# A product and a sum moved forward in the hand-written order of a group step (GFNet mixing and SwiGLU on one core)

## The chip, the cores and the metric

The kernel runs on one core of one Trainium2 chip, in fp32 throughout. The metric is the device time of one execution, in microseconds (us), as the median of several runs. Before the change it is 2811.93 us (three runs, 2810.69 to 2812.69).

## What is computed

Eight images of 3008 tokens and 256 channels are filtered along the token axis in the frequency domain, and each resulting token goes through a gated feed-forward block of width 1536.

```python
X = np.fft.rfft(x, axis=1)                       # x: 8 x 3008 x 256
y = np.fft.irfft(X * (filt_r + 1j * filt_i)[None], n=3008, axis=1)
t = y.reshape(24064, 256)
g = t @ w_gate                                   # 256 x 1536
out = (g * (1 / (1 + np.exp(-g))) * (t @ w_val)) @ w_out
```

## The kernel before

TensorE multiplies, and the other engines feed it. Each image (b, 0 to 7) is worked off in twelve group steps. A group step is one pair (k, g): k is one of four chunks of the image's tokens, g one of three thirds of the 1536 hidden channels. Ninety-six steps of 25 to 30 us each make up nearly all of the time.

**Inside a group step.** The tokens of a chunk are split in four blocks (0 to 3), and the products are saved by a scheme like Strassen's: instead of all block products, sums of blocks are multiplied and the results are recombined.

- P0 to P3 and Q0 to Q3 are the eight products of single blocks. Pi and Qi share one PSUM bank, k_i. Q0 opens bank k0 and P0 adds to it; so for blocks 0, 1 and 2, while P3 opens k3 and Q3 adds to it.
- A, B and E with two digits are products of sums of two blocks (18 of them), in banks a_ij and e_ij. Each product is two matmuls of 128x188, seen in the trace as four rows named wk, wa or we (line 1123); four W rows (wA, wF, wG, line 1220) are one of the seven output projections W1 to W7 of the group before.
- Between them come small operations. ScalarE copies: f_i (line 1138) is the negative of k_i after its first product, c_i (line 1142) is k_i after both, m (line 1158) copies an A bank, g and u (line 1165) are the Silu. VectorE: x and s (line 1145) form a bank's starting value from a k bank and an f (x03 and s13 both read k3, which P3 has opened; s13 writes the bank that A13 then adds to, s01 that of A01), y and e (line 1152, by the helper at line 327) do the like from a k bank and a c (e13 writes the bank that E13 adds to), l (line 1162, helper at line 323) subtracts, h and v (line 1170) multiply by the Silu, and o (helper at line 320, or ScalarE at line 1232) adds a finished projection to the output tile. GpSimd: D (differences of two f) and S (sums of hidden tiles for the projections).

**What sets the order.** SCHEDULE (lines 88 to 96) is the order of a group step, written out by hand: a list of tokens which the loop at line 1487 goes through once in each step, each token issuing its instructions to their engines. All are kept in the order of the program on their engine. A token with a prime (') belongs to the group of the step before. ORDER (line 107) picks the product tokens out of it and so sets in which slot of the weight tile each product's weights lie; PIECES (line 114) are the ranges of slots that are reloaded together, and the first holds slots 0 to 6, which end with Q2.

Between the products lie tokens of other work: t and i tokens (the last stage of the inverse transform for the next chunk, and output stores of image 0), x and z tokens (output stores and transposes), n tokens (sums of blocks for the next step), and b0 to b7, the eight parts of a burst: one piece of the spectrum of the image after. In images 1 to 6, steps 0 to 3 have a burst of the kind "quads" (line 733), steps 4 to 10 one of the kind "fours" (line 813), and the last step, in images 0 to 5, a "first_fold" (line 727). A burst's first parts put matmuls (wqa at line 743; wqc and wqb at lines 823 and 835) on TensorE between W2 and Q1; ScalarE copies their banks out (lines 754, 858 and 849), VectorE adds and subtracts (helpers at lines 320 and 323, line 853), SP and ScalarE store the result. Image 7 has no burst. Image 0 has instead the preparation of tables and weights, whose pieces are issued at fixed places of the list (tick_at, line 562).

Some work is tied to a token by name and goes where the token goes. For P0: keep_filter in steps 0 to 3 of image 1 (FILTER_AT, line 103), and in image 0 load_back in step 8 and reload_y in steps 3 to 8 (lines 1420 and 1424). All of these are DMA issues on SP.

Of the kernel before, what the change touches and what calls it, by code (L numbers as in the profile page):

```python
# [85 lines left out]


SCHEDULE = """
Q0 o3' z1.o' t4.2' W2 b0 f0 S00' S01' i0 b1 b2 x0.o' t0.0 x1.o' i1 Q1 t0.1 x2.o' P3 x3.o' f1 t4.3'
W1 x4.o' S10' x03 S11' D01 i2 i3 i4 s13 b3 x5.o' P1 o1 b4 t0.2 P0 o2 z0.o c1 i5 A13 g1 c0 S20' Q2  # L90
S21' g0 y01 m13 t1.0 h0 f2 s01 W6 t1.1 h1 x23 D02 P2 o6 D12 A01 t0.3 i6 c2 i7 B13 i8 g2 i9 n3' m01
i10 S30' t1.2 i11 x02 W7 S31' g13 y12 y02 B01 h13 o7 t1.3 t2.0 s02 s12 g01 h2 b5 Q3 t2.1 h01 e12
A02 y23 W4 e02 b6 y03 m02 g3 A12 o4 z2.o t2.2 E12 m12 B02 t2.3 l12 b7 E02 u12 e13 g02 t3.0 h3 s23
l02 B12 v12 E13 t3.1 h02 u02 A23 n2 l13 g12 v02 W5 s03 e23 h12 e01 m23 A03 o5 z3.o u13 E23 t3.2 m03
v13 E01 l23 e03 t3.3 t4.0 l01 u23 B23 v23 u01 E03 n1 t4.1 v01 g23 B03 l03 W3 h23 g03 u03 h03 v03
""".split()
# [1478 lines left out]
```

## Time and profile before

| quantity | value |
|---|---|
| median of three runs | 2811.93 us |
| profiled execution, device time | 2810.07 us |
| its span in the profile | 2808.3 us |
| TensorE clock granted | 0.999 |
| TensorE matmul rows | 15832 |
| mean row of wa, wk, we (128x188) | 323, 326, 323 ns |
| mean row of wA (128x376) | 481 ns |
| TensorE wk at line 1123 waiting for ScalarE's f | once, 1.7 us |
| TensorE wA at line 1220 waiting for VectorE's burst sum | three times, 1.9 us together |

The matmul rows overlap: one starts while the one before it still drains, so the distance from start to start, not the row's length, is what a product costs. Four rows of a product start 0.16 us apart in the unbroken parts, four rows of W 0.32 apart. In a timeline, rows of one kind that follow each other are joined ("x8" for two products of four), with their start, and the time from there to the end of the last. PEld rows are weight loads, which run beside matmuls. Behind the arrow in square brackets stands which work the engine waited for. "lent" is the name under which buffers of a shared room appear that a burst uses.

### The profile page before, as it was taken

Reading aid. Unit: us, or ns where it says so; the run is one execution under the profiler, and the core shown is the slowest. Engines: PE = TensorE matmul, PEld = TensorE weight load, DVE = VectorE, ACT = ScalarE, POOL = GpSimd, SP = SyncE. Lnnn points to the kernel's source line nnn. Section 1 sums busy time; section 2 is a strip of 40 time slices with the busy share of each in tenths; the row PEclk is TensorE's granted clock in tenths of the full one; section 3 lists DMA queues with packets and bytes.
Section 4 is the critical chain, followed back from the end, with each engine's and each line's share of the span. In section 5 each row is a group of like instructions: output and inputs, shape, how many; then the busy total and the mean of one; then the engine's idle time right before and its main releaser. Section 6 shows DMA issues by size and latency. Waiting matters only on the chain.

```text
span 2808.3 us, 49267 instructions
## 1 busy us (share of the span) xinstructions
PE 2773.1 (99%) x15832; PEld 2307.1 (82%) x15832; DVE 2048.3 (73%) x4675; ACT 1560.7 (56%) x4170; POOL 1580.9 (56%) x1689
## 2 busy tenths in 40 slices
PE   8999999999999999999999999999999999999998
PEld 6777888788888888888888888888888888888887
DVE  7888767777677766777767677777677767666666
ACT  5775455555555555555555555555555555555554
POOL 5886575465546565446554566455555455545544
PEclk9999999999999999999999999999999999999999
DMA  8778877777676776677767676668766677654543
GB/s 215 243 260 278 283 238 238 261 235 261 185 221 201 254 247 185 211 227 229 244 191 222 219 249 218 205 193 260 240 211 200 215 236 230 187 154 146 153 138 82
DMA packets 385272, 608.53 MB, mean 217 GB/s; under 512 B 198876, under 2 KB 268444, under 8 KB 384840
## 3 DMA queue, kind: packets, MB, share of 16 engines
q1 hardware_dynamic: 366202, 574.39, 65.2%
q10 hardware_dynamic: 16174, 25.50, 3.5%
q0 software_dynamic: 2640, 5.51, 0.8%
q8 instruction: 128, 2.10, 0.3%
q14 instruction: 128, 1.05, 0.1%
HBM read 484.65 MB, written 118.12 MB: 215 GB/s over the span
## 4 chain that ended last, share of the span: by engine, by line
PE 91%; POOL 2%; DVE 2%; ACT 1%; issue 1%; DMA 0%; POOLq 0%; ACTq 0%; DVEq 0%; SPq 0%
PE wa L1123 25%; PE wk L1123 17%; PE wA L1220 17%; PE we L1123 12%; PE wG L1220 8%; PE wF L1220 4%; PE pd L1026 3%; PE wqc L823 1%; PE wqb L835 1%; PE wqa L743 1%; POOL h L323 1%; POOL out_dram L1205 0%; PE pa L905 0%; PE pc L980 0%; DMA lent<-later_tbl 0%
## 5 line engine op out<-in xcount | busy, mean ns | idle before, releaser
L1123 PE MATMUL wa<-y_t,wt_t 128*128 128x188 f32 x4464 | 879.6, 323 | 5.0 <-ACT m L1158 2.4
L1123 PEld LDWEIGHTS wa<-y_t,wt_t 128*128 128x128 f32 x4464 | 745.9, 190 | 83.7 <-ACT wa L1149 9.5
L1123 PEld LDWEIGHTS wk<-y,wt_t 128*128 128x128 f32 x2976 | 494.1, 190 | 114.2 <-issue 34.0
L1123 PE MATMUL wk<-y,wt_t 128*128 128x188 f32 x2976 | 576.5, 326 | 2.1 <-ACT f L1138 1.7
L320 POOL TENSOR_TENSOR h<-h 128x376 f32<-128x376 f32 x190 | 182.9, 984 | 687.0 <-DVE h L1170 687.0
L323 POOL TENSOR_TENSOR h<-h 128x376 f32<-128x376 f32 x572 | 559.7, 1000 | 15.4 <-DVE h L320 15.2
L1220 PE MATMUL wA<-h,wo_t 128*128 128x376 f32 x1532 | 550.9, 481 | 5.9 <-DVE o L320 2.0
L1123 PE MATMUL we<-y_t,wt_t 128*128 128x188 f32 x2232 | 433.0, 323 | 2.1 <-ACT we L1154 1.5
L323 POOL TENSOR_TENSOR D<-f,f 128x376 f32<-128x376 f32 x288 | 280.9, 986 | 246.1 <-ACT f L1138 234.6
L323 DVE TENSOR_TENSOR we<-we,m 128x376 f32<-128x376 f32 x576 | 319.0, 555 | 125.1 <-ACT m L1158 60.9
L1123 PEld LDWEIGHTS we<-y_t,wt_t 128*128 128x128 f32 x2232 | 368.6, 190 | 6.1 <-DVE we L327 3.9
L1220 PEld LDWEIGHTS wA<-h,wo_t 128*128 128x128 f32 x1532 | 275.7, 190 | 113.9 <-POOL h L323 5.7
L1158 ACT COPY m<-wa 128x376 f32<-128x376 f32 x576 | 272.2, 473 | 83.5 <-PE wa L1123 79.6
L1165 ACT ACTIVATE u<-we 128x188 f32<-128x188 f32 x576 | 188.6, 327 | 171.7 <-DVE we L323 164.3
L1165 ACT ACTIVATE g<-wa 128x188 f32<-128x188 f32 x576 | 187.2, 326 | 164.8 <-PE wa L1123 158.1
L327 DVE SCALAR_TENSOR_TENSOR y<-wk,c 128x376 f32<-128x376 f32 x480 | 246.0, 538 | 40.3 <-ACT c L1142 23.0
L1220 PE MATMUL wG<-h,wo_t 128*128 128x376 f32 x768 | 274.0, 479 | 0.0
L1142 ACT COPY c<-wk 128x376 f32<-128x376 f32 x288 | 136.3, 473 | 212.8 <-PE wk L1123 212.8
L1154 ACT COPY we<-y 128x376 f32<-128x376 f32 x480 | 222.0, 480 | 18.8 <-DVE h L1170 13.9
L1138 ACT ACTIVATE f<-wk 128x376 f32<-128x376 f32 x288 | 139.9, 486 | 165.7 <-PE wk L1123 128.5
L1170 DVE TENSOR_TENSOR h<-wa,g 128x188 f32<-128x188 f32 x576 | 198.3, 345 | 34.8 <-ACT g L1165 34.5
L1170 DVE TENSOR_TENSOR h<-we,u 128x188 f32<-128x188 f32 x576 | 197.8, 344 | 28.9 <-ACT u L1165 17.5
(195 smaller groups left out, 3560.2 us busy)
## 6 DMA issues: line engine op xcount, KB each, us to landing
wt_t<-w_all SPq DMA_DIRECT2D x174, 896.0 KB
wt_t<-w_all SPq DMA_DIRECT2D x174, 768.0 KB
lent<-filter SPq DMA_DIRECT2D x36, 1024.0 KB
quads<-lent SPq DMA_DIRECT2D x96, 256.0 KB
d<-lent ACTq DMA_DIRECT2D x84, 256.0 KB
lent<-quads SPq DMA_DIRECT2D x144, 128.0 KB
lent<-raw SPq DMA_DIRECT2D x144, 128.0 KB
t<-d SPq DMA_DIRECT2D x114, 128.0 KB
```

The lines of the kernel that those rows point to most:

```text
L320: return eng.tensor_tensor(out=dst, in0=a, in1=b, op=ALU.add)
L323: return eng.tensor_tensor(out=dst, in0=a, in1=b, op=ALU.subtract)
L327: return nc.vector.scalar_tensor_tensor(out=dst, in0=a, scalar=-1.0, in1=b, op0=ALU.mult, op1=ALU.subtract)
L1026: pin(nc.tensor.matmul(out=rows, lhsT=self.t4[k, i][:, j, ts(cb, 128)], rhs=cols, start=j == 0, stop=True, skip_group_check=True))
L1123: pin(nc.tensor.matmul(out=ps[:, z], lhsT=self.wt[:, SLOT[p], z], rhs=rhs, start=start and z == 0, stop=True, skip_group_check=True))
L1138: pin(act.mul(self.small(f"f{i}", f"f{i}", 1), t[f"k{i}"], -1.0))
L1142: pin(act.copy(out=self.small(f"c{i}", f"c{i}", 1), in_=t[f"k{i}"]))
L1154: pin(act.copy(out=self.bank(f"e{at}"), in_=t[f"y{at}"]))
L1158: pin(act.copy(out=self.small(f"m{at}", "m", 4), in_=t[f"a{at}"]))
L1165: pin(act.activation(out=self.small(op, "g", 3, 1)[:, 0], in_=ps[:, 1], func=AF.Silu))
L1170: pin(v.tensor_tensor(out=dst, in0=ps[:, 0], in1=g, op=ALU.mult))
L1220: pin(nc.tensor.matmul(out=self.tiles[at], lhsT=wo_t[:, JB * q + i, WO[p], :], rhs=self.hs[i][:, HID[p]], start=start and i == 0, stop=Tru ...
```

## The change

Two tokens of SCHEDULE are moved; nothing else in the file differs. P0 goes from behind t0.2, where it followed P3, W1' and P1, to directly behind Q1 and so ahead of P3. e13 goes from behind b7, E02 and u12 to directly behind l12, ahead of the burst's last part b7.

```diff
-Q0 o3' z1.o' t4.2' W2 b0 f0 S00' S01' i0 b1 b2 x0.o' t0.0 x1.o' i1 Q1 t0.1 x2.o' P3 x3.o' f1 t4.3'
-W1 x4.o' S10' x03 S11' D01 i2 i3 i4 s13 b3 x5.o' P1 o1 b4 t0.2 P0 o2 z0.o c1 i5 A13 g1 c0 S20' Q2
+Q0 o3' z1.o' t4.2' W2 b0 f0 S00' S01' i0 b1 b2 x0.o' t0.0 x1.o' i1 Q1 P0 t0.1 x2.o' P3 x3.o' f1 t4.3'
+W1 x4.o' S10' x03 S11' D01 i2 i3 i4 s13 b3 x5.o' P1 o1 b4 t0.2 o2 z0.o c1 i5 A13 g1 c0 S20' Q2
...
-A02 y23 W4 e02 b6 y03 m02 g3 A12 o4 z2.o t2.2 E12 m12 B02 t2.3 l12 b7 E02 u12 e13 g02 t3.0 h3 s23
+A02 y23 W4 e02 b6 y03 m02 g3 A12 o4 z2.o t2.2 E12 m12 B02 t2.3 l12 e13 b7 E02 u12 g02 t3.0 h3 s23
```

The number of instructions is the same on every engine, and so are the PSUM banks. TensorE's products go Q0, W2', burst, Q1, P0, P3, W1', P1, A13, Q2 where they went Q0, W2', burst, Q1, P3, W1', P1, P0, A13, Q2. P0 adds to bank k0, which f0 reads after Q0 alone; so P0 must come after f0 has read it. The slots of P0, P3 and P1 in the weight tile change places within the first piece. On VectorE the order changes where b7 issues something there: e13 is then ahead of it.

## The prediction

> **What bounds the kernel now.** I read the page's busy table and chain of waits first, then TensorE's waits and those of its weight loads, then the timeline at one group step of each kind, and added up only what TensorE stands still for.
>
> ```profile
> PE 2773.1 (99%) x15832; PEld 2307.1 (82%) x15832; DVE 2048.3 (73%) x4675; ACT 1560.7 (56%) x4170; POOL 1580.9 (56%) x1689
> ...
> PE 91%; POOL 2%; DVE 2%; ACT 1%; issue 1%; DMA 0%; POOLq 0%; ACTq 0%; DVEq 0%; SPq 0%
> ```
>
> TensorE is busy for 99% of the span and is 91% of the chain. The change alters no instruction of it, so all that can move is where it stalls. The busy figure hides stalls of a few tenths; the weight loads' waits name them:
>
> ```profile
> PEld wa L1123 <- DVE wa L1145: 7.7, 17, 1.2
> ...
> PEld wk L1123 <- ACT lent L754: 6.3, 24, 0.4
> ...
> PEld we L1123 <- DVE we L327: 3.9, 14, 0.5
> ...
> PEld wk L1123 <- ACT f L1138: 2.8, 3, 1.9
> PEld wA L1220 <- PE wk L1123: 2.7, 3, 0.9
> ```
>
> The second row is P3 (24 steps: the four of images 1 to 6 whose bursts are quads) waiting until ScalarE has copied out the burst's bank. The third is E13 waiting for e13. The fifth (W1, three times) is on TensorE's own row 1.9 us put down to VectorE's burst sum of L320. The first is mostly A01 waiting for s01. These are idle times of the load queue, some of it cover for matmuls still running; the stall itself is read from starts. In a quads step (image 4):
>
> ```profile
> 1521.96 1.75 PE L1123 MATMUL wk<-y,wt_t 128*128 128x188 f32 x8
> 1522.16 1.07 ACT L754 COPY lent<-wqa 128x512 f32<-128x512 f32 x2 [1.89 <-PE wqa L743]
> 1522.80 0.61 PEld L1123 LDWEIGHTS wk<-y,wt_t 128*128 128x128 f32 x4 [0.23 <-ACT lent L754]
> 1523.54 1.43 PE L1220 MATMUL wA<-h,wo_t 128*128 128x376 f32 x4
> ```
>
> Q1 and P3 (the x8) take 1.58 us from start to W1's start (1521.96 to 1523.54). In image 7, which has no bursts, the same pair takes 1.27 (2478.20 to 2479.47), in a step with the other burst, a fours, 1.43 (1634.57 to 1636.00). And the far end of that same kind of step, here the first of image 4:
>
> ```profile
> 1470.91 0.80 PE L1123 MATMUL wk<-y,wt_t 128*128 128x188 f32 x4
> 1472.06 1.54 PE L1123 MATMUL wa<-y_t,wt_t 128*128 128x188 f32 x8 [0.35 <-DVE wa L1145]
> ```
>
> P2 needs 0.64 (half of 1.27), A01 starts 1.15 after it: a 0.51 us stall for s01. VectorE runs without a hole from 1465.08 (the burst's first subtraction) to the end of s01 at 1472.01. So in these steps VectorE, not TensorE, sets when A01 starts.
>
> **What the skill says.** "TensorE: Matmul & The Clock Gate" (Architectural detail) says TensorE's queue can pull weight loads ahead of running matmuls while VectorE and ScalarE are strictly first in, first out. The trace agrees: a product that never waited follows its predecessor at 0.64 us; one that waited pays about 0.10 more, since its second load was not ahead (E13 below: 0.75 to its successor). "PSUM — Partial Sum Buffer" (PSUM bank collisions raise a hardware error) says two engines must not be on one bank at once: hence P0, which adds into k0, must wait for f0's read of k0. The trace of before has no such wait in nearly all steps, since P0 came late.
>
> **The change, part by part.**
>
> P0 ahead of P3, fours (42 steps; in 30 of them, five of each image, ScalarE has three copies of the burst to make ahead of W1). Q1 to P1 takes 2.77 us (1634.57 to 1637.34) against 2.53 in image 7 (2478.20 to 2480.73). The excess of 0.24 holds 0.10 at Q1, which restarts behind the burst and keeps that, and 0.14 at W1, whose loads begin when ScalarE's second copy (L849) ends at 1635.96. P0 puts 0.64 of work ahead, so W1 no longer waits. 30 x 0.14 to 0.16 = 4.5 us less. What could take it back: P3, and with it x03 and s13, come 0.64 later. VectorE was busy until x03 at 1636.37, and P3 will end near 1636.60, so x03 moves by 0.4 to 0.5. s13 is still early for A13, and s01 would end at 1641.2 instead of 1640.78, with A01 at 1641.65: 0.4 of room. The saving stays.
>
> P0 ahead of P3, quads (24 steps). 1.58 less 1.27 less Q1's 0.10 is 0.21 of stall at P3; P0's 0.64 covers it: 24 x 0.21 = 5.0 us, first. But x03 starts no earlier: P3 ends near 1523.98 against the old 1523.5, so x03 starts at about 1524.25 instead of 1524.11, and VectorE's unbroken row to s01 moves 0.13 later. TensorE arrives 0.21 earlier at a wait that ends 0.13 later. In the first step of each image that is +0.13; in the third the room is 0.08 (s01 ends 1529.11, A01's loads begin 1529.17), so +0.15; in the second and fourth about 0 (Q2 behind an accumulator read, and A01, take it). 6 x 0.28 = +1.7 us net instead of -5.0.
>
> Steps 1 to 3 of image 1. Here W1 waits for VectorE's burst sum at a fixed time, 0.63 each (TensorE's row says 1.9 for three). P0 is done in that time: up to -1.9. VectorE's row is next; as TensorE was late here A01 has more room, so I take -1.6.
>
> e13 ahead of the last burst sum. In 14 quads steps E13 waits. In the third of image 4, A02 to E13 is 0.85 and E13 to its successor 0.75 (1537.53, 1538.38, 1539.13) where 0.64 each is due: 0.32 lost. VectorE did a 0.68 us subtraction (1537.18) just ahead of e13 (1537.78); with the two exchanged e13 ends 0.6 earlier, beyond the wait. In the first steps the loss is about 0.13, in image 1's two others 0.3 to 0.4: 6 x 0.32 + 6 x 0.13 + 0.75 = -3.4 us. The subtraction, later by e13's 0.55, serves a spectrum piece with no product behind it soon: 0. In steps whose last burst piece gives VectorE nothing, the order is the same: 0.
>
> The new wait. P0 needs f0, which ends at 1520.27 in the quads step, where P0 would start at 1522.7: no wait. Behind it on TensorE's queue are P3, W1, P1. The exception is the very first step: f0 starts only at 75.15 behind other work of ScalarE, where P3 used to fill the time. There Q0, Q1 end at 73.6, P0 waits to 75.6, and P3, x03, s13 and A13 follow: A13 at about 78.2 instead of 77.3: +0.9, bounds 0 and +1.5.
>
> What else moves with P0: its chores, a DMA issue on SP each (load_back once, reload_y in six steps of image 0, keep_filter four times). They pass the o store of x5.o' and loads and stores of the burst and of stage 3, which wait for work long done; the tiles they fill are free by then. 0, bounds -0.5 and +0.5. Preparation ticks of image 0 sit at fixed places of the list and so move by one token against P0's neighbours; its products otherwise have the same room: 0, bounds -1 and +1.5. Image 7: x03 and s13 0.64 later, with s01 ending 1.19 ahead of A01 (2483.99, 2485.18): 0.
>
> Sum: -4.5 + 1.7 - 1.6 - 3.4 + 0.9 = -6.9. The profiled execution took 2810.07 (span 2808.3 and 1.8 around it), 1.9 under the median of 2811.93. On the median: 2805.0 us, -0.25%.
>
> **Rivals.** Differences within 0.2% (5.6 us) are about what a measurement of this kernel can't tell from no change.
>
> Forecast (A): fours, E13 and image 1 gain, quads do not: 2805.0, own range 2801.5 to 2808.5. Chance 0.47, of which 0.37 is below 2806.3.
>
> B: the quads' gain stays too, because VectorE's row is looser than it looks (x03 does not move, or the transposes shift into a hole): a further -5.0 - 1.7, so 2798.3. Against it: no idle on VectorE in that stretch. 0.14.
>
> C: no change to be seen: the fours' 4.5 us go to the next wait, as in the quads, or E13's wait merely moves to a later E: 2809.5. For it: savings of a few tenths each, and VectorE at 73%. Against: the 0.4 of room. 0.24.
>
> D, slower: the later x03. It and s13, s01 behind it come 0.45 later in those 30 fours steps; if the true room at A01 is not 0.4 but nothing (a D01 of GpSimd or an output sum that moves along with W1, which also comes 0.5 later), A01 loses up to 0.2 to 0.4 with its restart of 0.10: 30 x 0.3 = +9.0 in place of -4.5, so 2805.0 + 4.5 + 9.0 = 2818.5. It decides once s01 comes more than 0.85 later (its margin of 1.01 less the 0.14 by which TensorE is earlier); about 0.5 is expected. 0.15.
>
> **Range and chances.** 2797 to 2816 takes in A, B, C and the nearer part of D, with the bounds of image 0; D's upper part and a B that also gains in image 0 are left out. Faster: 0.37 + 0.14 = 0.51. Same: 0.10 + 0.24 = 0.34. Slower: 0.15.
>
> **What would show it.** The row of P3 waiting for ScalarE's copy (6.3 us, 24) gone; W1's three waits (2.7) gone; the 14 waits of E13 gone; Q1 to P1 in a fours step at 2.53 + 0.10 + 0.64 = 3.27; A01's waits for s01 longer, the one at image 4's first step up from 0.51 to about 0.85, at its third a new one of 0.3 to 0.4; a new wait of P0 for f0 in the first step alone. Wrong would be: A01 or Q2 waits in fours steps or in image 7 (D), or unchanged A01 waits in the quads (B).

## The result and the profile after

Measured again side by side, sixteen runs each, the kernel before takes 2811.31 us and the changed one 2807.02 us in the median (2802.51 to 2812.23); the ratio is 0.9983, with a 95% interval of 0.9976 to 0.9989, or 3.1 to 6.7 us less. The forecast was 2805.0. The profiled execution of the changed kernel took 2803.6 us with a span of 2801.8, against 2810.07 and 2808.3.

In the page, TensorE's share has not changed, and its busy time has fallen with the span:

```profile
span 2801.8 us, 49322 instructions
...
PE 2767.8 (99%) x15832; PEld 2308.3 (82%) x15832; DVE 2048.7 (73%) x4675; ACT 1546.7 (55%) x4170; POOL 1579.7 (56%) x1689
```

The waits of the weight loads (total us, times, longest) show which stalls went and which came:

```profile
PEld wk L1123 <- issue: 40.4, 87, 0.8
...
PEld wk L1123 <- ACT f L1138: 10.3, 42, 1.9
PEld wa L1123 <- DVE wa L1145: 9.2, 17, 1.2
...
PEld wA L1220 <- PE wk L1123: 1.5, 3, 0.6
...
PEld we L1123 <- DVE we L327: 0.5, 1, 0.5
```

P3's 24 waits for ScalarE's copy are gone from the list. E13's are down from 3.9 us in 14 to 0.5 in one: the thirteen of the quads steps are gone, and the one left stands in image 0. W1's in image 1 are down from 2.7 to 1.5. In their place, the row that is mostly A01 waiting for s01 grew from 7.7 to 9.2 (by 0.08 in each of its eleven quads steps, the rest in image 0), and "wk <- issue" from 71 times to 87. Of the 42 idle times put down to f, one is P0's in the first step of image 0 (1.9). The other 41, about 0.21 each, stand ahead of P2's loads and cost nothing: P2 starts 1.26 us after W6, as in the kernel before.

The timeline of TensorE in a fours step of image 4, with Q1, P0 and P3, then W1, then P1 (start, duration, then the group):

```profile
1629.83 2.18 PE L1123 MATMUL wk<-y,wt_t 128*128 128x188 f32 x12
1631.85 1.43 PE L1220 MATMUL wA<-h,wo_t 128*128 128x376 f32 x4
1633.11 0.80 PE L1123 MATMUL wk<-y,wt_t 128*128 128x188 f32 x4
```

Q1, P0 and P3 (the x12) and W1 take 3.28 us from Q1's start to P1's. The kernel before took 2.77 without P0, and a product is 0.64, so 3.41 would be due had nothing been won: 0.13 less.

The first quads step of image 4, TensorE with A13, Q2, W6, P2 and A01:

```profile
1463.52 0.80 PE L1123 MATMUL wa<-y_t,wt_t 128*128 128x188 f32 x4
1464.29 0.88 PE L1123 MATMUL wk<-y,wt_t 128*128 128x188 f32 x4
1465.00 1.43 PE L1220 MATMUL wA<-h,wo_t 128*128 128x376 f32 x4
1466.27 0.80 PE L1123 MATMUL wk<-y,wt_t 128*128 128x188 f32 x4
1467.49 1.22 PE L1123 MATMUL wa<-y_t,wt_t 128*128 128x188 f32 x6 [0.43 <-DVE wa L1145]
```

A13 to Q2 takes 0.77 and Q2 to W6 0.71, where 0.64 each is due: the 0.21 that P3 no longer waits is spent again four products later, at Q2. Then P2 to A01 takes 1.22, so 0.58 of stall against 0.51 before. VectorE in the same stretch:

```profile
1461.82 0.55 DVE L1145 SCALAR_TENSOR_TENSOR x<-wk,f 128x376 f32<-128x376 f32 x1
1462.29 0.55 DVE L1145 SCALAR_TENSOR_TENSOR wa<-wk,f 128x376 f32<-128x376 f32 x1
1462.74 0.68 DVE L323 TENSOR_TENSOR lent<-lent,wqa 128x512 f32<-128x512 f32 x1
1463.45 0.69 DVE L320 TENSOR_TENSOR lent<-lent,wqa 128x512 f32<-128x512 f32 x1
...
1466.89 0.55 DVE L1145 SCALAR_TENSOR_TENSOR wa<-wk,D 128x376 f32<-128x376 f32 x1
```

The burst's second addition ends at 1464.14 and Q2 starts at 1464.29: Q2's bank is the one that the burst's second piece used, and it is free only when VectorE has added from it. s01 (the last row) ends at 1467.44, A01 starts at 1467.49.

The time of every group step, from its Q0 to the next, comes from the product rows of the two traces. In images 2 to 6 the differences are the same from image to image to within 0.02 us, apart from the twelfth step of some:

| steps | after less before, us |
|---|---|
| quads, first to fourth | -0.06, 0.00, +0.08, 0.00 |
| first fours step and seventh | 0.00, 0.00 |
| second to sixth fours step | -0.13 each |
| image 1, first four steps | -0.06, -1.06, -0.64, -0.64 |
| image 7, all | 0.00 |

From image 1's first product to the last matmul the changed kernel is 6.22 us shorter (2357.97 to 2351.75). In image 0 the sum is the same (370.54 and 370.55), though its steps are not, and ahead of that it is 0.28 shorter.

### The profile page after: what moved, and what is told of

Its sections match the earlier page's. It is cut to its first block, busy times and chain, and to the rows that moved or that the text cites. A ratio compares the mean times of both kernels' runs of the same rounds, so it can differ in the third digit from the quotient of the medians.

```text
span 2801.8 us, 49322 instructions
## 1 busy us (share of the span) xinstructions
PE 2767.8 (99%) x15832; PEld 2308.3 (82%) x15832; DVE 2048.7 (73%) x4675; ACT 1546.7 (55%) x4170; POOL 1579.7 (56%) x1689
## 4 chain that ended last, share of the span: by engine, by line
PE 90%; POOL 2%; DVE 2%; ACT 1%; issue 1%; DMA 0%; POOLq 0%; ACTq 0%; SPq 0%; DVEq 0%
PE wa L1123 25%; PE wk L1123 17%; PE wA L1220 16%; PE we L1123 12%; PE wG L1220 8%; PE wF L1220 4%; PE pd L1026 3%; PE wqc L823 1%; PE wqb L835 1%; PE wqa L743 1%; POOL h L323 1%; POOL out_dram L1205 0%; PE pa L905 0%; DVE we L323 0%; POOL D L323 0%
## 5 line engine op out<-in xcount | busy, mean ns | idle before, releaser
L323 POOL TENSOR_TENSOR h<-h 128x376 f32<-128x376 f32 x572 | 559.3, 998 | 15.1 <-DVE h L320 14.9
L320 POOL TENSOR_TENSOR h<-h 128x376 f32<-128x376 f32 x190 | 182.9, 983 | 673.9 <-DVE h L1170 673.9
L323 POOL TENSOR_TENSOR D<-f,f 128x376 f32<-128x376 f32 x288 | 280.6, 985 | 260.8 <-ACT f L1138 251.6
L323 DVE TENSOR_TENSOR we<-we,m 128x376 f32<-128x376 f32 x576 | 319.6, 556 | 124.8 <-PE we L1123 60.5
```

Of the source, the lines that this page charges most:

```text
L320: return eng.tensor_tensor(out=dst, in0=a, in1=b, op=ALU.add)
L323: return eng.tensor_tensor(out=dst, in0=a, in1=b, op=ALU.subtract)
```

## The experiments

Two theories stood against each other on where the gain at P3 and E13 went. V: VectorE's row, which a quads burst fills up to s01, sets Q2 and A01 and takes it back. K, later T: the saving is kept (K), or lost for reasons that have nothing to do with that row (T). "Images 1 to 7" is the time in each trace from image 1's first product to the last matmul, which is read more finely than the median; why is told at the end. The twelfth steps alone put up to 0.4 us into it that differ from trace to trace, so that column is not to be read below about half a microsecond.

| kernel | median, us | ratio to before, 95% interval | images 1 to 7, us | against before |
|---|---|---|---|---|
| before | 2811.31 to 2812.1 | | 2357.97 | |
| changed | 2807.02 | 0.9983 [0.9976, 0.9989] | 2351.75 | -6.22 |
| P0 alone | 2805.81 | 0.9982 [0.9976, 0.9989] | 2352.54 | -5.43 |
| e13 alone | 2810.38 | 0.9995 [0.9987, 1.0003] | 2356.55 | -1.42 |
| P0 behind P3 | 2808.25 | 0.9984 [0.9977, 0.9991] | 2351.92 | -6.05 |
| o2, z0 behind s01 | 2823.94 | 1.0049 [1.0035, 1.0063] | 2370.66 | +12.69 |
| x03 behind o6 | 2802.12 | 0.9969 [0.9957, 0.9981] | 2346.47 | -11.50 |
| the same, P0 behind P3 | 2803.78 | 0.9978 [0.9965, 0.9991] | 2348.71 | -9.26 |
| o2, z0 behind o6 | 2802.01 | 0.9961 [0.9948, 0.9973] | 2345.68 | -12.29 |
| x03, o2, z0 behind o6 | 2804.21 | 0.9968 [0.9956, 0.9980] | 2343.75 | -14.22 |

**P0 alone.**

```diff
-... i1 Q1 t0.1 x2.o' P3 x3.o' f1 t4.3'
+... i1 Q1 P0 t0.1 x2.o' P3 x3.o' f1 t4.3'
-... P1 o1 b4 t0.2 P0 o2 z0.o c1 ...
+... P1 o1 b4 t0.2 o2 z0.o c1 ...
```

> P0 moved, e13 left in its old place. My theory (V): the gain of the whole change sits in P0's move past W1. Against before: each of the 30 fours steps 0.13 us shorter (-3.9), steps 1 to 3 of image 1 0.64 shorter each (-1.9), quads steps of images 2 to 6 within 0.1 of before, since Q2 and A01, which wait for VectorE, take back the 0.21 saved at P3: about -5.5 us over the traces. In the first quads step of an image E13's 0.13 is still lost, so it is 0.08 longer than before. Rival (K): P3's saved wait is kept and e13's place undoes it elsewhere: quads steps 0.2 shorter, 24 x 0.21 = 5 us more, -10.5 in all.

Measured: fours -0.13 each, image 1's second to fourth steps -1.06, -0.65 and -0.64, quads steps +0.07, 0.00, +0.08, 0.00. V holds; K, which wanted 0.2 less in each quads step, falls. Image 1's second step gained 0.42 more than expected: there E13's wait went with P0's move alone. VectorE reached that step's l12 1.6 us earlier after its Q0 than before. An addition and a subtraction of the burst ahead of it, which had taken 1.39 and 1.02 us, took 1.03 and 0.76, and VectorE came to the first of them 1.0 earlier. In the kernel before, each began while GpSimd was at an operation of its own (VectorE, then GpSimd):

```profile
487.80 1.39 DVE L320 TENSOR_TENSOR lent<-lent 128x512 f32<-128x512 f32 x1
489.84 1.02 DVE L323 TENSOR_TENSOR lent<-lent 128x512 f32<-128x512 f32 x1
```

```profile
487.64 0.99 POOL L323 TENSOR_TENSOR h<-h 128x376 f32<-128x376 f32 x1
489.31 0.99 POOL L323 TENSOR_TENSOR h<-h 128x376 f32<-128x376 f32 x1
```

Both end 0.56 us after GpSimd's, as such pairs do in the whole trace (last section). With P0 moved, the subtraction meets only the end of GpSimd's operation (0.76), and the addition begins 0.84 ahead of it; why that one still takes 1.03 is open.

**e13 alone.**

```diff
-... t2.3 l12 b7 E02 u12 e13 g02 ...
+... t2.3 l12 e13 b7 E02 u12 g02 ...
```

> e13 moved, P0 left in its old place. V: E13's waits go in all 14 steps, but only the first quads step of each image is shorter for it (0.13); in the third the 0.32 saved comes back as a wait of A03 on ScalarE's chain of copies, which VectorE releases at the same time as before; image 1's second step 0.42 shorter, its third near 0. Sum about -1.2 us. Rival (K): the whole of what E13 waited is kept, -3.4 us (third steps 0.32 shorter).

Measured: first quads steps -0.13 or -0.14, third steps 0.00 (-0.02 in image 1), image 1's second -0.42. These are V's numbers. The expectation rested on the trace of the changed kernel, where the third quads step of image 4 reads so on TensorE (E13, A23, W5, A03 and the start of E23):

```profile
1533.55 0.80 PE L1123 MATMUL we<-y_t,wt_t 128*128 128x188 f32 x4
1534.18 0.80 PE L1123 MATMUL wa<-y_t,wt_t 128*128 128x188 f32 x4
1534.82 1.43 PE L1220 MATMUL wG<-h,wo_t 128*128 128x376 f32 x4
1536.30 0.91 PE L1123 MATMUL wa<-y_t,wt_t 128*128 128x188 f32 x4
1537.05 0.32 PE L1123 MATMUL we<-y_t,wt_t 128*128 128x188 f32 x1
```

and so on ScalarE:

```profile
1534.53 0.33 ACT L1165 ACTIVATE u<-we 128x188 f32<-128x188 f32 x1 [0.91 <-DVE we L323]
1534.75 0.91 ACT L1074 ACTIVATE y_t<-y 128x376 f32<-128x376 f32 x2
1535.56 0.32 ACT L1165 ACTIVATE g<-wa 128x188 f32<-128x188 f32 x1
1535.77 0.48 ACT L1149 COPY wa<-x 128x376 f32<-128x376 f32 x1
```

E13 now follows its predecessor without a stall, but W5 to A03 takes 1.48 where 1.26 is due, and A03 to E23 0.75: 0.32, just what E13 had lost. A03 waits for s03, the copy ending at 1536.25. In the kernel before, the same copy

```profile
1540.38 0.49 ACT L1149 COPY wa<-x 128x376 f32<-128x376 f32 x1
```

ended at 1540.87 and A03 started at 1541.03; it could have ended 0.1 later without holding A03 up. The copy does not come sooner in the changed kernel: ScalarE's row of u02, two sums for the next chunk, g12 and s03 begins when VectorE has done l02, and VectorE does e13 and the burst's subtraction in either order ahead of that.

**P0 behind P3.**

```diff
-... Q1 t0.1 x2.o' P3 x3.o' f1 t4.3'
+... Q1 t0.1 x2.o' P3 P0 x3.o' f1 t4.3'
-... b4 t0.2 P0 o2 ...
+... b4 t0.2 o2 ...
```

> P0 directly behind P3 and ahead of W1; e13 as before. P3 then still waits for ScalarE's copy in the quads steps. V (P3's saved wait is worth nothing): the same as P0 behind Q1, about -5.5 us: fours steps 0.13 shorter, steps 1 to 3 of image 1 0.64 shorter, quads steps as before to 0.02, with x03 not moved at all. K (P3's saved wait is worth its 0.21 to 0.34 a step): this kernel is 5 us slower than the one with P0 behind Q1.

Measured: fours -0.13, image 1's second to fourth steps -1.06, -0.65, -0.64, quads steps within 0.01 of before. By the traces it is 0.6 us shorter than with P0 behind Q1, not 5 us longer. So the fours gain needs P0 only ahead of W1. With VectorE's row as it is, taking away P3's wait buys nothing, and delaying x03 costs a little in the first and third step.

**o2 and the transpose behind s01**, in the changed kernel:

```diff
-... t0.2 o2 z0.o c1 ...
+... t0.2 c1 ...
-... f2 s01 W6 ...
+... f2 s01 o2 z0.o W6 ...
```

> The changed kernel, with o2 and the transpose z0 moved behind s01, so that VectorE's row up to s01 is 0.5 us (1.0 where there is a transpose) shorter. V (VectorE's row sets A01): A01's waits for s01 in the quads steps go; first steps 0.6 to 0.7 shorter, third 0.1, fourth 0.2: 6 x 0.9 = -5.5 us against the changed kernel, if no later wait takes it. Rival (T): A01's start is set by something else (GpSimd's D01, or VectorE's work that merely moves behind it, at x23 or y's): quads steps within 0.1 of the changed kernel.

A miss in its sum: against the changed kernel 0.13 to 0.76 longer in about every second step, 18.9 us over images 1 to 7. A01's waits did go in the quads steps (image 4's first, third and fourth: no stall left), as V has it, but W7 waits for o6, in image 7 too:

```profile
PE wA L1220 <- DVE o L320: 15.1, 31, 0.7
```

A timeline of that kernel on TensorE (A01 and B13, then W7), in the first step of image 7, and on VectorE:

```profile
2495.36 1.44 PE L1123 MATMUL wa<-y_t,wt_t 128*128 128x188 f32 x8
2497.32 1.50 PE L1220 MATMUL wA<-h,wo_t 128*128 128x376 f32 x4 [0.52 <-DVE o L320]
```

```profile
2494.87 0.54 DVE L320 TENSOR_TENSOR o<-o,wF 128x376 f32<-128x376 f32 x1
2495.44 0.58 DVE L1191 STREAM_TRANSPOSE o<-o 128x384 f32<-128x384 f32 x1
2495.94 0.32 DVE L1170 TENSOR_TENSOR h<-wk,g 128x188 f32<-128x188 f32 x1
2496.18 0.53 DVE L1145 SCALAR_TENSOR_TENSOR x<-wk,f 128x376 f32<-128x376 f32 x1
2496.64 0.53 DVE L320 TENSOR_TENSOR o<-o,wA 128x376 f32<-128x376 f32 x1
```

In steps without a burst VectorE had idle time ahead of y01 (1.19 us of it remain here), which o2 and the transpose used to fill; moved behind s01 they push o6 (the last row, ending at 2497.17), and W7 starts at 2497.32.

**An addition left out, before and with P0 behind Q1.** Both leave out VectorE's addition of the second piece of each quads burst, so a part of the spectrum is not summed. Of each there is one execution, the profiled one.

```diff
-            both(pieces[1])
+            both(pieces[1], False)
...
-                pin(add(nc.vector, t1[u][:, :, 0], t1[u][:, :, 0], views[u, 1]))
+                if second:
+                    pin(add(nc.vector, t1[u][:, :, 0], t1[u][:, :, 0], views[u, 1]))
```

> The kernel before, with VectorE's last addition of each quads burst (128x512, 0.69 us, one in each of 24 steps) left out, so that a part of the spectrum is not summed; all else in place. It is the base for the next kernel. V: A01's waits for s01 vanish, first quads steps about 0.5 to 0.6 shorter than before. T: no change.

> P0 behind Q1, e13 in its old place, and the same addition of VectorE left out (a part of the spectrum is not summed). Against the kernel before with the same left out. V: with 0.69 us of room on VectorE neither Q2 nor A01 can take back what P3 no longer waits, so the quads steps are 0.21 shorter (0.34 in the fourth), 5.8 us over the 24. Rival (T): the saving is taken back further on whatever VectorE does, and the quads steps of the two are alike to 0.05.

Measured: the first against the kernel before, -0.36 in the first quads step and -0.14 in the fourth (and -0.42 in image 1's second); A01 keeps 0.15 of wait in the first, which V had gone. The second against the first, in images 2 to 6: 0.00, -0.21, -0.21, -0.34, and -0.13 in the fours as ever. Where A01 no longer waits, P0 gives exactly what P3 used to lose; in the first step, where A01 still waits for s01, its wait grows from 0.15 to 0.36, and nothing is gained. That is V shown in one step and in its neighbours.

**x03 behind o6, with P0 behind Q1 and behind P3.** Here the whole computation is kept; x03, which nothing needs before s03, leaves the crowded row.

```diff
-... S10' x03 S11' D01 ...
+... S10' S11' D01 ...
-... P2 o6 D12 ...
+... P2 o6 x03 D12 ...
```

> The changed kernel with x03 moved behind o6, which takes 0.46 us off VectorE's row ahead of the burst's second piece, o1, y01 and s01 without adding anything ahead of o6. V: Q2 no longer waits in the quads steps (0.21 each, 0.27 in the fourth), and A01's wait shrinks or goes: against the changed kernel the first step of an image about 0.5 shorter, second 0.21, third 0.3 (less what A03 takes), fourth 0.4; x 6 = -8 us; fours steps and image 7 the same. Rival (T): what was saved at P3 is taken back later whatever VectorE's row does: quads steps within 0.1 of the changed kernel.

> As the last (x03 behind o6, e13 moved), but with P0 behind P3, so that P3 still waits for ScalarE's copy. V: once VectorE's row has room, P3's wait is worth what it takes: 0.21 in quads steps 1 to 3 and 0.34 in the fourth, so this kernel is slower than the one with P0 behind Q1 by up to 24 x 0.24 = 5.8 us. T: the two are alike in the quads steps.

TensorE in the first quads step of image 4, A13, Q2 and W6, with P0 behind Q1:

```profile
1462.89 0.80 PE L1123 MATMUL wa<-y_t,wt_t 128*128 128x188 f32 x4
1463.53 0.80 PE L1123 MATMUL wk<-y,wt_t 128*128 128x188 f32 x4
1464.17 1.43 PE L1220 MATMUL wA<-h,wo_t 128*128 128x376 f32 x4
```

Measured, against the changed kernel: -0.31, -0.21, -0.29, -0.24 in the quads steps of images 3 to 6, and 0.00 in the fours and in image 7. In image 2 the first step is 0.04 longer instead, and in image 1 the first alone gains. Q2 waits no more, save 0.03 at its second pass in the fourth step; A01 still waits 0.48 in the first step and 0.11 in the fourth. So it is 5.3 us and not the 8 that V expected. With P0 behind P3 instead, the second to fourth steps of images 2 to 6 are 0.21, 0.19 and 0.09 longer, and the first is the same. So P3's wait is worth its 0.2 where VectorE's row has room. Where A01 still waits for that row it is worth nothing (first step) or 0.09 (fourth); V had put 0.21 and 0.34 there. The medians, 2802.12 and 2803.78, lie in the same order, but their intervals overlap.

**o2 and the transpose behind o6, and both moves together.**

```diff
-... t0.2 o2 z0.o c1 ...
+... t0.2 c1 ...
-... P2 o6 D12 ...
+... P2 o6 o2 z0.o D12 ...
```

> The changed kernel with o2 and the transpose z0 moved behind o6 and not only behind s01. The kernel with them behind s01 lost 0.16 (o2) to 0.75 (with the transpose) a step where W7 waited for o6. V: with o6 ahead of them W7's wait is gone and A01's too: first steps 0.6 to 0.7 shorter than in the changed kernel, third 0.1, fourth 0.2, Q2's waits unchanged, others the same: about -5 us. Rival: x02, y12 and y02, which now come later, hold up A02 or E12 in their place, and the time is not below that of the changed kernel.

> Both moves: x03, o2 and the transpose behind o6. V: Q2's and A01's waits all gone, first steps 0.9 shorter than in the changed kernel, others as with x03 alone: -9 to -10 us. Rival: VectorE has then 1.6 us more behind o6, and o7 or A02 waits in its place: slower than with x03 alone.

Measured, against the changed kernel, in images 2 to 6: -0.70, 0.00, -0.10, -0.22 in the quads steps and 0.00 in the rest; both together -0.90, -0.21, -0.08, -0.43, and +0.05 where a transpose meets no quads burst (one step of image 2 is 0.17 longer). In image 1 the first step gains as in the others, but the second to fourth gain nothing, and with both moves the third is 0.23 longer; so both moves bring 8.0 us over images 1 to 7, where V expected 9 to 10. With o6 ahead of it, W7 does not wait. The rival for both moves was right only in those 0.05 and in the third step, where A03 waits 0.45 instead of 0.22. By the medians either move alone, or both, is faster than the kernel before, at 0.9961 to 0.9969 of it. Against the changed kernel's 0.9976 to 0.9989 only the interval of o2 and z0 behind o6 lies apart, the other two overlap with it. Which of the three is best the medians do not tell; by images 1 to 7 of the traces it is both, and all three are below the changed kernel by 5.3 to 8.0 us.

## Why the prediction was right, and where it was not

The sign and most of the mechanism were right. That the size was right too, in the trace, is in part luck: some terms were not, and erred both ways. By the medians the gain is 0.15 to 0.17%, a little under the 0.2% above which I had put the better half of the chances.

- Fours, -4.5: right. 30 x 0.13 = -3.9. A01's room was put at 0.4; in the trace of after x03 starts 0.42 us later in the step, and s01 ends 0.46 us ahead of A01's start, about 0.4 before it would hold it up. Rival D, which needed that room to be nothing, did not happen.
- Quads, +1.7 in place of -5.0: right in kind. P0 alone gave +0.07, 0, +0.08, 0 in four steps: 6 x 0.15 = +0.9. Forecast too large because x03 moved by 0.06 and not by 0.13. The place was partly wrong: A01's wait in the first step was to grow from 0.51 to 0.85 and came to 0.58, and the new one in the third was to be 0.3 to 0.4 and came to 0.1, as Q2 took the 0.21 in all four steps; I had named Q2 for the second and fourth only.
- Image 1, -1.6: too small. P0 alone gave 1.06 + 0.65 + 0.64 = -2.35, of which 0.42 is E13's wait, counted by me under e13. The rest is P0's whole 0.64 in each of three steps; nothing took a part of it back. W1's waits were to be gone and are only shorter.
- e13, -3.4: this is the step that failed. Alone it took away the waits of all thirteen quads steps (the fourteenth of the list is in image 0 and stays), but only 6 x 0.13 and image 1's 0.42 came out as time, and the last is contained in what P0 gives, so that in the change it adds -0.8. The prediction said that the subtraction moved behind e13 costs "0", since no product waits for it, and did not ask what stood next behind E13: A03, which in the trace of before had 0.1 us to spare. The sum itself was also too large: 6 x 0.32 already holds the third step of image 1, which the 0.75 counts again, so the waits came to 3.1. (The product ahead of E13 that the prediction calls A02 is B12; its times are right.)
- First step of image 0, +0.9: the mechanism came as described, the size did not. Counted from the step's Q0, P0 waits 1.60 for f0, A13 0.62 for s13, and TensorE is 0.8 late at Q2. At A01 it is only 0.17 late: the filler matmuls on the way wait for VectorE's h, and that wait fell from 1.2 to 0.6 us. The step ends 0.18 later. P0 alone gives +0.19 there and e13 alone -0.01, so this is P0's; with P0 behind P3 the same step is 0.90 shorter than before.
- Chores on SP, the ticks, image 7: 0 to the second digit in image 7. For image 0 the equal sum shows little: step 8 is 0.74 shorter and step 11 0.44 longer, and the kernel with the addition left out, whose image 0 has the order of before, differs from it by 0.52 in step 8.

For images 1 to 7 the parts add up: -3.9 + 0.9 - 2.35 - 0.8 = -6.15, against -6.22 in the trace, of which -0.1 is in twelfth steps. Forecast and trace agree (-6.9 and -6.5 in the span) because errors cancel: 3.2 us too much gain in e13 and the fours, against 2.3 too little in the quads, image 1 and the first step. That the medians show 4.3 is within the interval, which 6.2 is too. Whether the 2 us between them are chance or a cost ahead of image 1 is not shown: one profile of each kernel can't tell, as the opening and image 0 spread by more (below).

Of the rivals, B (the quads keep their gain) is refuted by P0 alone, and its reason confirmed from the other side: with room on VectorE the gain does stay. C was right for the quads and for E13's wait in the third steps, which "merely moves", but to an A product.

## What to carry to other kernels

A wait removed on the bound engine was worth here only the slack of the next wait that another engine sets. So follow the row of the engine that releases it up to the next two or three products, and subtract. When an operation is moved out of a full stretch of a helper engine, put it behind the last operation on which the bound engine waits, not merely behind the next: the same two operations cost 18.9 us behind s01 and gained 6.1 behind o6, each against the changed kernel. And in a kernel whose steps repeat, compare step by step in the traces: here that resolved hundredths of a microsecond where the medians resolved microseconds.

## What the runs showed beside this

- The opening varies by about as much as this change is worth. From the start to the first product it took 69.9 to 76.4 us in the twelve profiles (of twelve kernels, one each), image 0 from 370.5 to 376.1, while images 2 to 7, apart from the twelfth steps, repeat to 0.01 or 0.02 us where nothing was changed. The changed kernel's runs spread over 9.7 us. In the three profiles whose first product came last (74.5 to 76.4), TensorE's granted clock was 0.50 from about 70 us on, for 7 to 10 us, and so when that product came; in the other nine it was full then. What made it fall was not looked into.
- A product that waits for one semaphore starts 0.05 us after its releaser's end (A01 after s01: 1467.44 to 1467.49) and pays about 0.10 at its second pass; Q2 in the first step of image 4, which waits for VectorE and for a TensorE row at once, started 0.15 after the addition, though the TensorE row was long done, and paid 0.08.
- VectorE's additions and subtractions of two tiles of the burst's room (lent<-lent, 128x512, L320 and L323) came out longer beside GpSimd. In the trace of before, 76 of the 77 that began with no sum or difference of GpSimd under way took 0.67 to 0.69 us (one 0.79). All 19 that began during one took 0.83 to 1.39 and ended 0.55 or 0.56 us after GpSimd's end. Those that read one operand from a PSUM bank (lent<-lent,wqa) began during one 54 times and took 0.67 to 0.69 each time. The times coincide throughout; no experiment moved GpSimd's work.
